# Loading the first two x tiles as two short-row loads instead of one long-row load, with one dummy product fewer and w2 in one load

## The chip, the cores and the metric

The kernel runs on one core of one Trainium2 chip. The metric is the device time of one execution in microseconds (us). Times are medians of several executions; beside them stand profiles of single executions, whose span runs from the first to the last instruction and is about 1.8 us shorter than the device time. The kernel before took 179.77 us (median of 3, 179.62 to 179.87).

## The reference, cut to what matters

For 2048 tokens of width 512 the output is `g * a + (1 - g) * b`. Here `g` is a sigmoid gate, `a` is linear attention over 32 heads, and `b` is a gated feed-forward block. The change touches only the start of the attention branch.

```python
x = A_x                                      # 1 x 2048 x 512, bf16
qkv = x @ wqkv                               # q, k, v
pq, pk = phi(q), phi(k)                      # phi(t) = where(t > 0, t + 1, exp(t)) + 1e-6
kv = einsum("bhsd,bhse->bhde", pk, v)        # sum over ALL tokens
z  = einsum("bhsd->bhd", pk)
# ... a = (pq @ kv) / (pq . z) @ wo ;  b = (silu(x @ w1) * (x @ w3)) @ w2
```

The sum over all tokens comes first: nothing of the output can be finished before k of every token has been computed and accumulated. So the kernel begins with x, its transpose xT, and the key weights wk.

## The kernel before

The kernel cuts the tokens into 16 tiles of 128. For tiles 0 and 1, TensorE transposes x through PSUM, and VectorE and ScalarE copy the result into xT. All other tiles get xT from transposing loads. While the first loads are under way, TensorE runs dummy products.

```python
    TF = 2
    x_first = x2d[0 : TF * P, :].rearrange("(p j) d -> p j d", j=TF)    # 2 KB rows: tokens 2p, 2p+1
    out_first = out2d[0 : TF * P, :].rearrange("(p j) d -> j p d", j=TF)
    dq.dma_start(out=x_sb[:, 0:TF, :], in_=x_first)                     # dq is the SP queue
    nc.scalar.dma_start(out=wk_sb[:, 0:2, :], in_=wqkv_r[:, 0:2, D : 2 * D])
    dq.dma_start(out=wk_sb[:, 2:4, :], in_=wqkv_r[:, 2:4, D : 2 * D])
    ...
    dq.dma_start(out=xT[:, :, TF * P : TB], in_=x2d[TF * P : TB, :], transpose=True)   # tiles 2, 3
    for tb in range(1, NTB):
        dq.dma_start(out=xT[:, :, tb * TB : (tb + 1) * TB], in_=..., transpose=True)
        x_ts = slice(TF if tb == 1 else tb * TPB, (tb + 1) * TPB)
        dq.dma_start(out=x_sb[:, x_ts, :], in_=x_r[:, x_ts, :])
    # ... then wq, the small weights, wv, w1, w3, wo
    for fcs in (slice(0, FC // 2), slice(FC // 2, FC)):
        dq.dma_start(out=w2_sb[:, fcs, :], in_=w2_r[:, fcs, :])
    ...
    emit_warm(TB, TB, TB, TB, TB, TB, P, P, P)      # dummies: six 512 wide, three 128 wide
    ...
    emit_xT(0)                                      # four transposes and two copies per tile
    emit_xT(1)
    for kc, t in ((0, 0), (1, 0), (0, 1), (1, 1), (2, 0), (3, 0)):
        emit_k_mm(k0[t], t, kc)                     # kc 0, 1: first half of wk; 2, 3: second half
    # ... rest of k of tiles 1 to 3 (16 products in all), then XP products and k of tiles 4 to 15 in turn
```

An "XP product" is the first use of k: it accumulates x against phi(k). From the first XP product on, TensorE has work all the time (in the profile it is busy for all of 9 to 173 us).

## Time and profile before

| What | Before | Where it is read |
|---|---|---|
| time | 179.77 us | executions |
| TensorE (PE) busy | 174.3 of 177.9 us | the page, part 1 |
| x landed, wk's first and second half landed | 3.62, 4.29, 5.29 us | single records of the trace: last semaphore update of each load |
| first k product, first XP product | 4.53, 8.94 us | the timeline |
| pitch of the 512-wide products, start to start | 0.427 us, from 6.46 us on 0.216 us | single records; the trace's clock record begins at 6.455 us |

These are lines of the page: span, busy time of each engine, the granted clock in 40 slices, and the engines' shares of the chain of waits that ended last.

```profile
span 177.9 us, 2476 instructions
...
PE 174.3 (98%) x883; PEld 84.2 (47%) x883; DVE 118.7 (67%) x204; ACT 65.5 (37%) x123; POOL 63.7 (36%) x80
...
PEclk9999999999999999999999999999999999999999
...
PE 98%; DVE 0%; issue 0%; DVEq 0%
...
```

TensorE bounds the kernel: it is 98% of the chain. The clock row says 9 in every slice, although the trace's own clock record begins only at 6.455 us. What precedes the first record is drawn as full speed (the first slice, up to 4.4 us, says 9 while the pitch there is 0.427 us), so the early state of the clock has to be read from the pitch of the products.

The next lines are the timeline of the first 10 us. Columns are start, duration (with merged neighbours), engine, line, operation, operands and count. "ACTq" and "SPq" are the instants at which a load is issued.

```profile
...
0.80 0.47 ACTq L83 DMA_DIRECT2D wk_sb<-in_A_wqkv_dram  x1
...
0.81 0.40 SPq L82 DMA_DIRECT2D x_sb<-in_A_x_dram  x1
...
0.84 3.04 PE L162 MATMUL warm<-const-bfloat16-1.0 128*128 128x512 bf16 x9 [0.84 <-PEq L495]
...
1.26 0.42 SPq L84 DMA_DIRECT2D wk_sb<-in_A_wqkv_dram  x1
...
1.73 1.31 SPq L87 DMA_TRANSPOSE xT<-in_A_x_dram  x1
...
3.67 1.06 PE L175 MATMUL xTp<-ident,x_sb 128*128 128x128 bf16 x8
...
4.53 4.58 PE L185 MATMUL k<-wk_sb,xT 128*128 128x512 bf16 x16
...
6.36 0.58 SPq L96 DMA_DIRECT2D x_sb<-in_A_x_dram  x1
...
8.94 1.03 PE L205 MATMUL XP<-pk_sb,x_sb 128*128 128x512 bf16 x4
...
```

The dummies hand over to the transposes at 3.67, just after x landed, and the transposes to the k products at 4.53. The table of waits of TensorE and the busy time of the stretch from 4 to 6 us follow.

```profile
...
PE warm L162 <- PEq L495: 0.8, 1, 0.8
```

### The profile page before, as it was taken

To read this page: it belongs to the slowest core of one execution; us is meant where nothing else is said; L and a number is where in the kernel's file an instruction comes from. 1 tells how busy PE (TensorE), PEld (TensorE's weight loads), DVE (VectorE), ACT (ScalarE), POOL (GpSimd) and SP (SyncE) were. 2 spreads that over 40 slices of the span, in tenths; PEclk is the share of its full clock that TensorE was granted. 3 is DMA by queue.
4 is the path that set the end of the run, shared out by engine and by line. 5 is a ranking of instruction groups with operands and counts; after the bars stand their busy time and mean duration, and the time that the engine had idled before them with its cause. 6 is when DMAs were issued, how large, how long until landed. Compare 5 with 4: busy or idle time off the path is not lost.

```text
span 177.9 us, 2476 instructions
## 1 busy us (share of the span) xinstructions
PE 174.3 (98%) x883; PEld 84.2 (47%) x883; DVE 118.7 (67%) x204; ACT 65.5 (37%) x123; POOL 63.7 (36%) x80
## 2 busy tenths in 40 slices
PE   8999999999999999999999999999999999999993
PEld 4444444474444545444454544444545444444463
DVE  0397667899999837498786375978754669776000
ACT  3542323476532333343333333242433323341222
POOL 6087765689154323262003232720032328000000
PEclk9999999999999999999999999999999999999999
DMA  5999999901005011123000111240001022200001
GB/s 169 205 306 284 291 332 371 335 18 29 10 1 116 0 44 33 44 59 88 0 0 11 37 37 37 60 90 6 0 7 63 10 66 63 59 0 0 29 34 58
DMA packets 30252, 15.14 MB, mean 85 GB/s; under 512 B 20672, under 2 KB 30112, under 8 KB 30240
## 3 DMA queue, kind: packets, MB, share of 16 engines
q1 hardware_dynamic: 29968, 14.72, 30.2%
q10 hardware_dynamic: 272, 0.26, 0.4%
q8 instruction: 7, 0.11, 0.3%
q14 instruction: 5, 0.04, 0.1%
HBM read 8.42 MB, written 2.10 MB: 59 GB/s over the span
## 4 chain that ended last, share of the span: by engine, by line
PE 98%; DVE 0%; issue 0%; DVEq 0%
PE o_ps L360 19%; PE up_ps L321 19%; PE gate_ps L313 19%; PE o_ps L351 8%; PE q_ps L218 8%; PE XP L205 8%; PE k_ps L185 6%; PE r_ps L242 3%; PE k L185 2%; PE o_ps L355 2%; PE warm L162 2%; PE kvT_ps L437 1%; PE W_ps L455 0%; PE xTp L175 0%; DVE o_out L369 0%
## 5 line engine op out<-in xcount | busy, mean ns | idle before, releaser
L321 PE MATMUL up_ps<-xT,w_sb 128*128 128x512 bf16 x160 | 41.1, 379 | 0.0
L313 PE MATMUL gate_ps<-xT,w_sb 128*128 128x512 bf16 x160 | 41.1, 379 | 0.0
L226 POOL TENSOR_TENSOR qz<-pq,z_sb 128x512 f32<-128x512 bf16 x16 | 18.5, 1164 | 58.1 <-DVE pq L146 58.0
L326 ACT ACTIVATE th<-gate_ps 128x512 bf16<-128x512 f32 x40 | 23.9, 597 | 39.0 <-PE gate_ps L313 37.5
L360 PE MATMUL o_ps<-w_sb,hT 128*128 128x512 bf16 (+3 forms) x180 | 37.5, 355 | 0.0
L328 DVE SCALAR_TENSOR_TENSOR gs<-th,gate_ps 128x512 bf16<-128x512 bf16 x40 | 27.2, 681 | 5.4 <-ACT th L326 5.1
L333 DVE TENSOR_TENSOR hT<-up_ps,gs 128x512 bf16<-128x512 f32 x40 | 27.6, 691 | 3.8
L143 DVE TENSOR_SCALAR phi_m<-phi_e 128x512 bf16<-128x512 bf16 x32 | 13.6, 425 | 21.8 <-ACT phi_e L141 21.6
L360 PEld LDWEIGHTS <-hT 128*128 128x128 bf16 x180 | 16.9, 98 | 17.8
L321 PEld LDWEIGHTS <-w_sb 128*128 128x128 bf16 x160 | 15.7, 98 | 18.9
L313 PEld LDWEIGHTS <-w_sb 128*128 128x128 bf16 x160 | 15.6, 98 | 18.6
L365 ACT ACTIVATE o_out<-o_ps,omg 128x512 bf16<-128x512 f32 (+2 forms) x17 | 11.2, 659 | 30.6 <-PE o_ps L360 30.6
L293 POOL TENSOR_TENSOR pqn<-pq,rden 128x512 bf16<-128x512 bf16 x16 | 16.6, 1056 | 15.0 <-DVE rden L286 13.1
L195 POOL TENSOR_TENSOR pks<-pks,pk_sb 128x512 f32<-128x512 f32 x15 | 17.4, 1161 | 7.4 <-DVE pk_sb L146 6.7
L351 PE MATMUL o_ps<-W_sb,pqT 128*128 128x512 bf16 (+3 forms) x72 | 16.8, 355 | 0.0
L218 PE MATMUL q_ps<-wq_sb,xT 128*128 128x512 bf16 x64 | 16.4, 379 | 0.0
L205 PE MATMUL XP<-pk_sb,x_sb 128*128 128x512 bf16 x64 | 16.3, 379 | 0.0
L229 DVE TENSOR_REDUCE den<-qz 128x32 f32<-128x512 f32 x16 | 10.9, 684 | 7.9 <-POOL qz L226 7.8
L141 ACT ACTIVATE phi_e<-k_ps 128x512 bf16<-128x512 f32 x12 | 7.2, 597 | 14.4 <-PE k_ps L185 14.4
L141 ACT ACTIVATE phi_e<-q_ps 128x512 bf16<-128x512 f32 x16 | 9.6, 597 | 7.8 <-PE q_ps L218 7.8
L185 PE MATMUL k_ps<-wk_sb,xT 128*128 128x512 bf16 x48 | 12.3, 379 | 0.0
L146 DVE SCALAR_TENSOR_TENSOR pq<-q_ps,phi_m 128x512 bf16<-128x512 f32 x16 | 11.1, 691 | 0.5
(59 smaller groups left out, 119.8 us busy)
## 6 DMA issues: line engine op xcount, KB each, us to landing
w_sb<-in_B_w_dram SPq DMA_DIRECT2D x6, 640.0 KB, 8.5
out_dram<-o_out SPq DMA_DIRECT2D x15, 128.0 KB, 1.7
x_sb<-in_A_x_dram SPq DMA_DIRECT2D x2, 512.0 KB, 3.9
x_sb<-in_A_x_dram SPq DMA_DIRECT2D x1, 768.0 KB, 5.1
wq_sb<-in_A_wqkv_dram SPq DMA_DIRECT2D x1, 512.0 KB, 5.1
wv_sb<-in_A_wqkv_dram SPq DMA_DIRECT2D x1, 512.0 KB, 6.3
wo_sb<-in_A_wo_dram SPq DMA_DIRECT2D x1, 512.0 KB, 9.6
wk_sb<-in_A_wqkv_dram ACTq DMA_DIRECT2D x1, 256.0 KB, 3.5
```

Source lines behind the costliest of these rows:

```text
L185: nc.tensor.matmul(k_ps[:], lhsT=xT[:, kc, t * P : (t + 1) * P], rhs=wk_sb[:, kc, :], start=(kc == 0), stop=(kc == KC - 1),)
L195: nc.gpsimd.tensor_add(pks[:], pks[:], pk_sb[:, t, :])
L205: nc.tensor.matmul(XP_ps[dc][:], lhsT=x_sb[:, t, dc * P : (dc + 1) * P], rhs=pk_sb[:, t, :], start=(t == 0), stop=(t == NT - 1),)
L218: nc.tensor.matmul(q_ps[:], lhsT=xT[:, kc, ts_tok], rhs=wq_sb[:, kc, :], start=(kc == 0), stop=(kc == KC - 1),)
L226: nc.gpsimd.tensor_tensor(out=qz[:], in0=st[tb, "pq"][:, tt, :], in1=z_sb[:], op=ALU.mult)
L313: nc.tensor.matmul(gate_ps[:], lhsT=w1_sb[:, kc, fsl], rhs=xT[:, kc, tok_sl], start=(kc == 0), stop=(kc == KC - 1),)
L321: nc.tensor.matmul(up_ps[:], lhsT=w3_sb[:, kc, fsl], rhs=xT[:, kc, tok_sl], start=(kc == 0), stop=(kc == KC - 1),)
L326: nc.scalar.activation(out=th[:], in_=gate_ps[:], func=ACT.Tanh, scale=0.5)
L328: nc.vector.scalar_tensor_tensor(out=gs[:], in0=th[:], scalar=1.0, in1=gate_ps[:], op0=ALU.add, op1=ALU.mult)
L333: nc.vector.tensor_tensor(out=st[tb, "hT"][:, fc, :], in0=up_ps[:], in1=gs[:], op=ALU.mult)
L351: nc.tensor.matmul(o_ps[:], lhsT=st[tb, "pqT"][:, c, tsl], rhs=W_sb[:, c, a:b], start=(c == 0), stop=False,)
L360: nc.tensor.matmul(o_ps[:], lhsT=st[tb, "hT"][:, fc, tsl], rhs=w2_sb[:, fc, a:b], start=False, stop=(fc == FC - 1),)
```

## The change

The intent is to let TensorE start on tile 0 while tile 1 is still in flight, in natural token order, so that the output needs no special row order. One dummy is dropped because work comes sooner, and w2 becomes one load. The diff, cut to its core:

```diff
-    dq.dma_start(out=x_sb[:, 0:TF, :], in_=x_first)
+    for t in range(TF):
+        dq.dma_start(out=x_sb[:, t, :], in_=x_r[:, t, :])
...
-    for fcs in (slice(0, FC // 2), slice(FC // 2, FC)):
-        dq.dma_start(out=w2_sb[:, fcs, :], in_=w2_r[:, fcs, :])
+    dq.dma_start(out=w2_sb[:], in_=w2_r)
...
-    emit_warm(TB, TB, TB, TB, TB, TB, P, P, P)
+    emit_warm(TB, TB, TB, TB, TB, P, P, P)
...
-                rows = out_first[t] if t < TF else out2d[t * P : (t + 1) * P, :]
+                rows = out2d[t * P : (t + 1) * P, :]
```

More of the change, by code (lines that the diff above doesn't have):

```diff
@@ L79 @@
     TF = 2
-    x_first = x2d[0 : TF * P, :].rearrange("(p j) d -> p j d", j=TF)
-    out_first = out2d[0 : TF * P, :].rearrange("(p j) d -> j p d", j=TF)
-    dq.dma_start(out=x_sb[:, 0:TF, :], in_=x_first)
+    for t in range(TF):
+        dq.dma_start(out=x_sb[:, t, :], in_=x_r[:, t, :])
     nc.scalar.dma_start(out=wk_sb[:, 0:2, :], in_=wqkv_r[:, 0:2, D : 2 * D])
```

## The prediction

> **What bounds the kernel.** TensorE. The page has PE busy 174.3 of 177.9 us (98%), and the chain that ended last is 98% PE. No wait of a matrix product is listed except the 0.8 us before the first dummy. From about 9 us on, products follow each other every 0.216 us (the chain: four in 0.86 us). So only the head, before that stream, can move the time. The stores of tiles 0 and 1 and the w2 loads are off the chain: w2 is issued at 24.4 us, lands some 8.5 us later and is first used near 58 us.
>
> **The head before** (single records of the trace). Dummies run from 0.84 us, 0.427 us apart; the last narrow one starts at 3.57. The x load is issued at 0.81 and its last semaphore update lands at 3.62; the first transpose's weight load starts at 3.66, so nothing is idle. Eight transposes take 0.107 each; the first k product starts at 4.53. Its wk half landed at 4.29; the other half lands at 5.29 and is used at 6.24. Pitch is 0.427 us until about 6.45 us and 0.216 us after: the clock was released there, although the page's clock row shows 9 in every slice. [...] So k products started earlier than 6.45 us run at half speed: moving the head by d moves the end by d/2.
>
> **What changes.** One wide dummy fewer: -0.427 us, so the dummies end near 3.25 instead of 3.68. Tile 0's load is half as large. In the packets, 2 KB took 84 ns and 1 KB 46 ns, the first up to 0.6 us; the slow engines should end tile 0 near 2.72, and with 0.35 to 0.4 us from semaphore packet to landing it is there at about 3.1: in time for 3.25. Tile 1 is issued 0.45 us later, and I expect its packets after wk's first half (from the ACT queue): before, wk's second half, issued at 1.26, sent nothing until 3.71, when the ACT queue's packets ended. [...] Estimate for slow engines: 2.72 + 16x0.046 + 8x0.046 + 0.4 = 4.2 us. So PE transposes tile 0 at 3.25 to 3.68, idles about 0.55 us, transposes tile 1 at 4.25 to 4.68 and starts k at 4.68, 0.15 us later than before. Half of it counts: +0.07 us. wk's first half would land earlier (near 3.9) and help nothing; the second half and the transposing loads come about as before. w2 in one load and contiguous stores of tiles 0 and 1: 0.
>
> **Prediction.** 179.85 us, 8 in 10 within 179.6 to 180.4. Faster by over 2%: 0.005; within 2%: 0.985; slower by over 2%: 0.01.
>
> **What would show it.** Landing of x tile 0 near 3.1 and of tile 1 near 4.2, after wk's first half; a PE gap of about 0.5 us between the fourth and fifth transpose; first k product near 4.7; pitch change still at 6.4 to 6.5; from 10 us on the same stream, shifted by under 0.1 us; w2 lands long before 58 us.
>
> **What would make it wrong.** [...] (2) Tile 1's packets go before wk's: it lands near 3.6, k starts with wk at about 4.3, and the kernel is 0.1 us faster; chance 0.3. (3) A later transposing load for tiles 2 and 3 (slack about 0.35 us at 7.0 us) opens a small gap.

## More of the kernel before

Behind "4.00:6.00" and the length stand the busy times of PE, PEld, DVE, ACT and POOL, then clock, DMA share and GB/s.

```profile
...
4.00:6.00 2.00, 2.00 (x11) 1.12 (x10) 0.58 (x2) 0.77 (x2) 0.00 (x0) 1.00 1.16 250
...
```

PE waits only for its start, and the DMA queues moved 250 GB/s in that stretch.

## The result, and the profile after

The changed kernel took 179.58 us (median of 6, 179.26 to 179.97), the kernel before 179.69 us (median of 6, 179.01 to 179.89). The ratio is 1.000 with a 95% interval of 0.9978 to 1.0022: the same. A ratio here is the mean time of one kernel's fast runs over that of the other's in the same rounds, so it is not quite the ratio of the medians quoted.

The same parts of the page, after:

```profile
span 178.0 us, 2458 instructions
...
PE 173.0 (97%) x866; PEld 83.8 (47%) x882; DVE 118.7 (67%) x204; ACT 65.5 (37%) x123; POOL 63.9 (36%) x80
...
PEclk9999999999999999999999999999999999999999
...
PE 94%; DMA 3%; issue 1%; SPq 0%; DVE 0%; DVEq 0%
...
```

The chain now holds 3% of DMA: 2.5% is the load of wk's second half. (PE counts 17 products fewer, but PEld only one weight load fewer, which is the dummy: the other 16 are records missing from the trace.) The timeline of the changed kernel:

```profile
...
0.80 0.46 ACTq L82 DMA_DIRECT2D wk_sb<-in_A_wqkv_dram  x1
...
0.81 0.87 SPq L81 DMA_DIRECT2D x_sb<-in_A_x_dram  x2
...
0.84 2.61 PE L160 MATMUL warm<-const-bfloat16-1.0 128*128 128x512 bf16 x8 [0.84 <-PEq L493]
...
1.73 0.43 SPq L83 DMA_DIRECT2D wk_sb<-in_A_wqkv_dram  x1
...
2.19 1.69 SPq L86 DMA_TRANSPOSE xT<-in_A_x_dram  x1
...
3.25 0.63 PE L173 MATMUL xTp<-ident,x_sb 128*128 128x128 bf16 x4
...
4.20 0.61 PE L173 MATMUL xTp<-ident,x_sb 128*128 128x128 bf16 x4 [0.32 <-DMA x_sb<-in_A_x_dram]
...
4.60 1.50 PE L183 MATMUL k<-wk_sb,xT 128*128 128x512 bf16 x4
...
6.27 2.92 PE L183 MATMUL k<-wk_sb,xT 128*128 128x512 bf16 x12 [0.17 <-DMA wk_sb<-in_A_wqkv_dram]
...
6.99 0.58 SPq L95 DMA_DIRECT2D x_sb<-in_A_x_dram  x1
7.29 1.41 PEld L183 LDWEIGHTS <-xT 128*128 128x128 bf16 x8 [0.49 <-DMA xT<-in_A_x_dram]
...
```

The transposes fall into two groups of four (3.25 and 4.20), the k products into a group of four at 4.60 and the other twelve from 6.27, and the weight load for the ninth k product starts only at 7.29. The table of waits names three:

```profile
...
PE warm L160 <- PEq L493: 0.8, 1, 0.8
PE xTp L173 <- DMA x_sb<-in_A_x_dram: 0.3, 1, 0.3
PE k L183 <- DMA wk_sb<-in_A_wqkv_dram: 0.2, 1, 0.2
```

The same stretch from 4 to 6 us shows that the DMA queues slowed down just there, to 135 GB/s:

```profile
...
4.00:6.00 2.00, 1.80 (x8) 0.95 (x9) 0.29 (x1) 0.69 (x2) 0.00 (x0) 1.00 1.18 135
...
```

| Step (us) | Before | Predicted | After |
|---|---|---|---|
| x tile 0 landed / tile 1 landed | 3.62 together | 3.1 / 4.2 | 3.09 / 4.15 |
| wk's first half landed | 4.29 | 3.9 | 3.79 |
| first k product | 4.53 | 4.68 | 4.60 |
| wk's second half landed | 5.29 | about as before | 6.23 |
| xT of tiles 2 and 3 landed | 6.64 | about as before | 7.25 |
| pitch changes | 6.46 | 6.4 to 6.5 | 5.55 |
| first XP product | 8.94 | about 9.0 | 9.03 |
| last PE instruction minus first XP product | 165.99 | same | 165.99 |

The first XP product is where I had put it, but not by my sum: that it came out right was luck. The pitch changed 0.9 us earlier than before, a gain of about 0.45 us, and TensorE stood still for wk (0.34 us) and xT (0.16 us), a loss of about the same size. The last row says that nothing after the first XP product changed: neither w2 in one load nor the output rows cost or gave anything.

### The profile page after: what moved, and what is told of

Same layout as the page of the kernel before. It is cut to its first block, busy times and chain, and to the rows that moved or that the text cites. A ratio compares the mean times of both kernels' runs of the same rounds, so it can differ in the third digit from the quotient of the medians.

```text
span 178.0 us, 2458 instructions
## 1 busy us (share of the span) xinstructions
PE 173.0 (97%) x866; PEld 83.8 (47%) x882; DVE 118.7 (67%) x204; ACT 65.5 (37%) x123; POOL 63.9 (36%) x80
## 3 DMA queue, kind: packets, MB, share of 16 engines
HBM read 8.42 MB, written 2.10 MB: 59 GB/s over the span
## 4 chain that ended last, share of the span: by engine, by line
PE 94%; DMA 3%; issue 1%; SPq 0%; DVE 0%; DVEq 0%
PE o_ps L358 19%; PE up_ps L319 19%; PE gate_ps L311 19%; PE o_ps L349 8%; PE XP L203 8%; PE q_ps L216 8%; PE k_ps L183 6%; PE r_ps L240 3%; DMA wk_sb<-in_A_wqkv_dram 3%; PE o_ps L353 2%; PE k L183 2%; PE kvT_ps L435 1%; PE W_ps L453 0%; SPq L81 0%; DVE o_out L367 0%
```

## The experiments

Twelve runs of nine kernels were made. All gave correct results. Those of one job shared a chip and the runs of the kernel before.

### The kernel before against itself, and the changed kernel again

Theory P: the instant of the pitch change (call it R) is not the kernel's own. Rival K: it follows the kernel's work. Theory C: the DMA stall comes with the change. Rival A: it was an accident of one execution. Neither kernel was edited.

> The kernel before, unchanged, run against itself: what two sets of the same program differ by. Theory P (phase): the moment at which the pitch of the products falls from 0.427 to 0.216 us does not belong to the kernel; it was 6.455 us in the profile of before and 5.548 us in that of after, and it will be elsewhere again here, by up to a few us, while x lands at 3.6 and the first k product starts at 4.53 as before. Rival K (kernel): the moment follows the kernel's own work, and it is again 6.45 us within 0.05. Time: ratio 1.000, within 0.3%.

> The changed kernel, unchanged. In its profile the second half of wk landed at 6.23 us (5.29 before) because packets of the transposing load stood for up to 1.38 us, and PE waited 0.34 us for wk and 0.16 us for xT. Theory C: that stall comes with the change (wk third on the SP queue, the transposing load right behind it), so wk's second half lands after 6.0 us again. Rival A (accident): it lands near 5.3 us and no packet of the first transposing load takes over 0.5 us. In both: x tile 0 lands near 3.1, tile 1 near 4.15, first k product near 4.6. Time: ratio to before 1.000 within 0.3% under A; up to 0.3% slower under C when the pitch changes early.

Measured: the kernel before against itself took 179.45 us (6 runs) against 178.94 us (11 runs), ratio 1.0017 (0.9993 to 1.004). So the same program differs from itself by half a microsecond in its medians on one chip. The changed kernel took 179.63 us, ratio 1.0031 (1.0013 to 1.005). Timelines of TensorE, the kernel before first:

```profile
...
3.89 1.03 PE L175 MATMUL xTp<-ident,x_sb 128*128 128x128 bf16 x8
4.72 4.10 PE L185 MATMUL k<-wk_sb,xT 128*128 128x512 bf16 x16
8.65 1.03 PE L205 MATMUL XP<-pk_sb,x_sb 128*128 128x512 bf16 x4
...
```

```profile
...
3.25 0.63 PE L173 MATMUL xTp<-ident,x_sb 128*128 128x128 bf16 x4
4.36 0.61 PE L173 MATMUL xTp<-ident,x_sb 128*128 128x128 bf16 x4 [0.48 <-DMA x_sb<-in_A_x_dram]
4.76 3.80 PE L183 MATMUL k<-wk_sb,xT 128*128 128x512 bf16 x16
8.40 1.03 PE L203 MATMUL XP<-pk_sb,x_sb 128*128 128x512 bf16 x4
...
```

R lay at 5.68 us in the first and 5.13 us in the second. It had been 6.46 in the first profile of before, and it came earlier although the kernel's own work came later (x landed at 3.84 instead of the expected 3.6, k at 4.72 instead of 4.53): P stands and K falls. The clock records also show a grid. The time from the release of the clock (granted share 1.0 from 6.455 us in before) to the fall at the end (share 0.5 from 177.122 us) is 170.666 us in before, and 174.079 us in after and in both kernels here; these differ by 3.413 us and are 50 and 51 times 3.4133 us. So in these four profiles both changes of the clock lie on one grid of 3.4133 us, and as the same program met it at different instants (R at 6.46 and 5.68 us), the kernel does not set it. One step of this grid, 3.413 us, is called a window below.

With R known, the head can be summed. A k product started before R takes 0.427 us, one after R 0.216 us, and there are 16. So the first XP product starts at `R + 3.453 - 0.506 * (R - k)`, where k is the first k product, if PE waits for nothing in between (if R comes before k, at `k + 3.453`):

| Profile | k | R | sum | measured | PE waits |
|---|---|---|---|---|---|
| before | 4.53 | 6.46 | 8.93 | 8.94 | none |
| before, second | 4.72 | 5.68 | 8.65 | 8.65 | none |
| after | 4.60 | 5.55 | 8.52 | 9.03 | 0.34 for wk, 0.16 for xT |
| after, second | 4.76 | 5.13 | 8.40 | 8.40 | none |

The waits of "after" here are gaps between product starts in single records: the fifth started at 6.27 instead of 5.94, the ninth at 7.29 instead of 7.13. The sum holds to 0.01 us, and what it lacks is exactly the waits. The second profile of the changed kernel shows no stall. Its wk landed at 5.29, its xT at 6.43, and the stretch from 4 to 6 us moved 265 GB/s:

```profile
...
4.00:6.00 2.00, 1.64 (x9) 0.95 (x10) 0.29 (x1) 0.69 (x2) 0.00 (x0) 1.00 1.20 265
...
```

So the stall is not in every execution, as rival A said; whether the change makes it more frequent was still open.

### The split alone, and the dummy alone

```diff
 # the split alone: the kernel before with
-    dq.dma_start(out=x_sb[:, 0:TF, :], in_=x_first)
+    for t in range(TF):
+        dq.dma_start(out=x_sb[:, t, :], in_=x_r[:, t, :])
 # (and the output rows of tiles 0 and 1 in natural order)
 # the dummy alone: the kernel before with
-    emit_warm(TB, TB, TB, TB, TB, TB, P, P, P)
+    emit_warm(TB, TB, TB, TB, TB, P, P, P)
```

> The kernel before with the x load split alone: six wide dummies and two w2 loads stay. The dummies end near 3.68, so tile 0 is transposed at 3.68 to 4.1 although it landed near 3.1; tile 1 lands near 4.15 and is transposed at once; first k product near 4.6, as in the changed kernel. So if tile 1's landing is the bound, keeping the dummy costs nothing: same time as the changed kernel (within 0.1 us at the same moment of the pitch change). If the dummies were the bound instead, k would start near 5.0.

> The kernel before with one wide dummy fewer alone. x lands at 3.62 as before, so PE stands idle from about 3.25 to 3.66 and the first k product starts at 4.53 as before: the dummy was filler, 0.00 us. If idleness counted against the clock, the pitch change would come at least a window of about 3.4 us later than in a run of before with the same phase (k products still 0.427 us apart at 8 us).

The dummy alone: 179.19 us, ratio 1.0012 (0.9993 to 1.0032). Its TensorE timeline:

```profile
...
0.84 2.61 PE L162 MATMUL warm<-const-bfloat16-1.0 128*128 128x512 bf16 x8 [0.84 <-PEq L495]
3.85 1.04 PE L175 MATMUL xTp<-ident,x_sb 128*128 128x128 bf16 x8 [0.40 <-DMA x_sb<-in_A_x_dram]
4.68 4.36 PE L185 MATMUL k<-wk_sb,xT 128*128 128x512 bf16 x16
...
```

From the end of the dummies (3.25, by the starts of the products) to the first transpose (3.85) PE idled 0.60 us: 0.43 for the missing dummy, the rest because x landed only at 3.81 in this execution (3.62 was expected). The transposes began at once, and the k products followed them without a pause. The second profile of the kernel before, where x landed at 3.84, has its first k product at 4.72, so the missing dummy cost nothing: it was filler. By the starts of the products the pitch changed at about 6.2 us, so 0.60 us of idleness did not hold the clock back here.

The split alone: 180.10 us, ratio 1.0064 (1.0043 to 1.0084), the slowest of the four and not as expected. Its timeline has three stalls and a fourth at 12.7 us:

```profile
...
3.68 0.48 PE L174 MATMUL xTp<-ident,x_sb 128*128 128x128 bf16 x4
4.31 0.40 PE L174 MATMUL xTp<-ident,x_sb 128*128 128x128 bf16 x4 [0.15 <-DMA x_sb<-in_A_x_dram]
4.54 1.04 PE L184 MATMUL k<-wk_sb,xT 128*128 128x512 bf16 x4
5.79 1.02 PE L184 MATMUL k<-wk_sb,xT 128*128 128x512 bf16 x4 [0.20 <-DMA wk_sb<-in_A_wqkv_dram]
7.03 1.90 PE L184 MATMUL k<-wk_sb,xT 128*128 128x512 bf16 x8 [0.22 <-DMA xT<-in_A_x_dram]
8.77 1.03 PE L204 MATMUL XP<-pk_sb,x_sb 128*128 128x512 bf16 x4
...
```

```profile
...
12.72 1.04 PE L204 MATMUL XP<-pk_sb,x_sb 128*128 128x512 bf16 x3 [0.34 <-DMA x_sb<-in_A_x_dram]
```

The first k product started at 4.54, as expected, and R was 3.86, very early. The sum would put the first XP product at 8.00; it started at 8.77. The fourth stall, for x of tiles 2 to 7, cost another 0.5 us: from the first XP product to the last PE instruction it took 166.50 us instead of 165.99. All four are late loads.

Single DMA records show what they have in common. A 256-byte packet of a transposing load takes 0.018 us (the median over the first 9 us in before and in after). In the two profiles with the stall so far, and in a third one below, many packets of the first transposing load took over 0.5 us, and they ended together, about 0.2 us after the last packet of wk's second half (in after they took 0.59 to 1.38 us):

| Profile | packets over 0.5 us | the longest | all ended between | wk's last packet ended |
|---|---|---|---|---|
| after | 19 | 1.38 us | 5.97 and 6.01 us | 5.80 us |
| after, third | 22 | 1.01 us | 5.78 and 5.83 us | 5.60 us |
| the split alone | 14 | 0.90 us | 5.52 and 5.56 us | 5.36 us |

In after, 13 of 16 semaphore packets of wk's second half had gone out by 4.44 us, but all but one of their updates arrived only from 6.04 us on. Their load was late too (xT of tiles 2 and 3 landed at 7.25 us in after, at 6.64 in before). Why these packets took so long was not shown. In the first profile of before the updates of wk's second half also came bunched, from 5.05 us on, 0.2 us after its last packet (4.83 us). So what differs in the stalled profiles is how late the last packets of wk's second half are: in after, its last three semaphore packets went out at 4.88, 5.62 and 5.80 us. In the other profiles of this job, and in the first one of before, no such packet took longer than 0.35 us.

### Which part makes the split slow: dummy or w2

```diff
 # the changed kernel with
-    emit_warm(TB, TB, TB, TB, TB, P, P, P)
+    emit_warm(TB, TB, TB, TB, TB, TB, P, P, P)
 # w2 alone: the kernel before with
-    for fcs in (slice(0, FC // 2), slice(FC // 2, FC)):
-        dq.dma_start(out=w2_sb[:, fcs, :], in_=w2_r[:, fcs, :])
+    dq.dma_start(out=w2_sb[:], in_=w2_r)
```

> The changed kernel with the sixth wide dummy put back (so: split x loads and one w2 load). On the last chip the split alone (six dummies, two w2 loads) took 180.1 us against 179.6 of the changed kernel and 178.9 of before. Theory D: the dummy makes the difference between those two, so this one takes as long as the split alone, 0.6% over before. Rival W: the single w2 load makes it, so this one is as fast as the changed kernel, 0.3% over before. Rival L (lag): neither does; what costs is one engine that starts the second half of wk late, behind which all packets of the first transposing load stand. Then the profile shows, when slow, packets of that load above 0.5 us, xT of tiles 2 and 3 after 6.9 us and a PE wait for it, and when fast, none.

> The kernel before with w2 in one load alone. w2 is issued after 24 us, lands in the thirties and is first used near 58 us, so 0.00 us: ratio 1.000 within 0.2%, and PE without a gap from 12 to 58 us. Theory W of the run above would need this to be faster by 0.2 to 0.3%.

The changed kernel with six dummies took 179.39 us against 179.64, ratio 1.0001 (0.9973 to 1.003). w2 alone took 179.39 us, ratio 0.9999 (0.9973 to 1.0026). Neither profile has a stall (wk landed at 5.13 and 5.34), and both have 165.99 us behind the first XP product. Theory D (the dummy) falls. Theory W (w2) would have needed w2 alone to be faster; it was not. Theory L, a lag in some executions, is what is left, by elimination and not by a test: the split alone was 0.6% over before in both its sets, this kernel, which differs from it in the w2 load only, in its one set was not, and a joint effect of the split and the two w2 loads was not ruled out (w2 is issued at 24 us, long after the head).

### The order of the first loads

```diff
 # tile 1 on the ACT queue: the changed kernel with
-    for t in range(TF):
-        dq.dma_start(out=x_sb[:, t, :], in_=x_r[:, t, :])
+    dq.dma_start(out=x_sb[:, 0, :], in_=x_r[:, 0, :])
+    nc.scalar.dma_start(out=x_sb[:, 1, :], in_=x_r[:, 1, :])
 # one load of short rows: the kernel before with
-    dq.dma_start(out=x_sb[:, 0:TF, :], in_=x_first)
+    dq.dma_start(out=x_sb[:, 0:TF, :], in_=x_r[:, 0:TF, :])
 # (and the output rows of tiles 0 and 1 in natural order)
```

> The changed kernel with tile 1 issued from the ACT queue, before wk's first half; on the SP queue wk's second half and the transposing loads come one issue (0.46 us) sooner. Theory O (order): tile 1 lands near 3.5 instead of 4.15 to 4.3, because nothing stands before it; wk's first half lands near 4.2 and now bounds, first k product near 4.3 (4.6 to 4.76 in the changed kernel); SP issues as in before. Rival: the ACT queue's packets come as late as they did for wk, after those of x tile 0 and wk's second half, and tile 1 lands after 4 us again. Time: as before or up to 0.15 us less at the same moment of the pitch change; against the changed kernel 0.2 to 0.5 us less if its cost was the SP queue's order.

> The kernel before with one x load in natural token order: 256 rows of 1 KB instead of 128 of 2 KB, one issue. Tells the size of the rows from the number of loads. By the packet times (46 ns for 1 KB, 84 for 2 KB) the load takes 16 x 46 instead of 8 x 84 ns per engine, 0.06 us more: lands near 3.7, first k product at 4.6, time +0.03 us, within 0.1% of before. If short rows are what makes an engine lag, packets of the first transposing load stand for over 0.5 us here too and the time is 0.3 to 0.6% over before, as with the split.

Tile 1 on the ACT queue took 181.80 us, ratio 1.0115 (1.0077 to 1.0153), so the expectation of a faster kernel was a miss. Its tile 1 landed at 3.79 and tile 0 at 3.61, together nearly as late as the one long-row load. wk's first half, now second on the ACT queue, landed last of all, at 5.63, after the second half at 5.44, and the first k product started at 5.67. TensorE stood idle for 1.3 us. Five of its six executions took 181.5 to 182.0 us; the profiled one took 179.8, with R at 4.22 (three packets of its first transposing load took 0.51 to 0.56 us).

One load of short rows took 180.05 us, ratio 1.0026 (1.0001 to 1.0052). It landed at 4.27 instead of the expected 3.7; wk's packets on the ACT queue went out among its own from 2.3 us on. It had no lag (no packet of the first transposing load above 0.42 us). Its sum, with k at 5.15 and R at 6.31, gives 9.18, and 9.18 was measured. So short rows cost 0.6 us here where the packet times said 0.06; that the other queue's load took its share in between is the likely reason, and was not tested apart.

### All of the head on one queue, and repeats

```diff
 # the changed kernel with
-    nc.scalar.dma_start(out=wk_sb[:, 0:2, :], in_=wqkv_r[:, 0:2, D : 2 * D])
+    dq.dma_start(out=wk_sb[:, 0:2, :], in_=wqkv_r[:, 0:2, D : 2 * D])
```

> The changed kernel with wk's first half on the SP queue too, so that nothing competes: x tile 0, x tile 1, wk first half, wk second half. Theory Q: tile 1 was late because the ACT queue's wk packets went between the two tiles. Then tile 1 lands near 3.5, wk's halves near 4.2 and 5.2, first k product near 4.3, and no engine starts late (no packet of the first transposing load over 0.5 us). Everything behind on the SP queue is issued one more issue (0.46 us) later, so xT of tiles 2 and 3 may land near 6.8 and be waited for when the pitch changes early. Time: within 0.15% of before; if the 0.46 us per issue is what costs, 0.1 to 0.3% slower than before.

> Tile 1 on the ACT queue once more, one look. Five of its six executions took 181.5 to 182.0 us, the profiled one 179.8 with the pitch change at 4.22 us and a PE gap of 1.1 us before the first k product. Theory G (gap): in the slow ones the gap kept the clock from being released, and the pitch changes one window later. If this execution is slow (over 181), its k and first XP products stand 0.427 us apart until after 7 us. Rival: it is slow by a DMA that lands 2 us late, with the pitch change before 6.5 us as elsewhere.

With all four loads on the SP queue, tile 0 landed at 2.93 and tile 1 at 3.40: theory Q about their order is right. All eight transposes ran at once. But wk's first half landed at 5.24 instead of 4.2: twelve of its 16 semaphore updates had arrived by 4.48, the last four came from 4.87 on. Two packets of the first transposing load took 0.56 us, where none over 0.5 was expected. So late parts of a load occur here too, with no other queue in between, and why stays open. The time was 181.41 us, ratio 1.0104 (1.0067 to 1.014), with executions in two groups: 179.8 and 180.0, and four at 181.4 to 182.0. The profiled execution was one of the slow group (181.52). TensorE's timeline:

```profile
...
3.25 1.06 PE L173 MATMUL xTp<-ident,x_sb 128*128 128x128 bf16 x8
5.28 5.72 PE L183 MATMUL k<-wk_sb,xT 128*128 128x512 bf16 x16 [0.97 <-DMA wk_sb<-in_A_wqkv_dram]
10.84 1.03 PE L203 MATMUL XP<-pk_sb,x_sb 128*128 128x512 bf16 x4
...
```

TensorE idled from 4.10 to 5.28, and its 16 k products then took 5.72 us against 4.58 before: R was 9.58. On the grid, the clock could have been released one window earlier, at 6.17, but the 3.413 us up to there held the gap of 1.18 us. By the sum, R at 6.17 gives a first XP product at 9.17; it started at 10.84, so 1.7 us later. The repeated look at tile 1 on the ACT queue, meant to catch a slow execution of that kernel, caught a fast one (179.56 us, R at 3.94), so for that kernel the cause of the slow group is likely the same but was not recorded.

From the profiles one can read how busy TensorE was in the window that ended at R and in the one before it (share of 3.413 us between product starts, idle gaps taken out):

| Profile | R | last window | window before it |
|---|---|---|---|
| before | 6.46 | 1.00 | 0.64 |
| after | 5.55 | 0.85 | 0.38 |
| after, second | 5.13 | 0.80 | 0.25 |
| after, third | 3.65 | 0.81 | 0.00 |
| all on SP | 9.58 | 1.00 | 0.66 |

In these profiles a window with 0.80 sufficed and one with 0.66 did not. The shares count the transposes: the 0.80 of "after, second" would be 0.56 without them, and it released the clock, while the 0.64 of before, dummies alone, did not. Transposes started 0.107 us apart before R (before) and about 0.06 us after it (the split alone, 4.31 to 4.49 us). The gap between the two tiles was 0.52 us in the first profile of the changed kernel and 0.69 us in the second, where it leaves 0.80: enough, but not by much.

> The split alone once more (six dummies, two w2 loads): 0.64% over before on one chip, while the same with w2 in one load showed 0.0% on another. Theory L (an engine that lags in some executions, or on some chips): the ratio is anywhere from 1.000 to 1.006, and goes with the profile: packets of the first transposing load over 0.5 us when slow, none when fast. Rival D/W (program): 0.6% over before again.

> The changed kernel a third time, beside the split alone on the same chip: theory L says that the two differ by no more than the lag does, so within 0.3% of each other if neither or both lag. First XP product, by the sum found so far (moment of the pitch change + 3.453 - 0.506 x (that moment - first k product)) within 0.02 us unless PE waits for wk or xT.

In the last job, the split alone took 180.01 us, ratio 1.0055 (1.0033 to 1.0077), and the changed kernel 179.85 us, ratio 1.0045 (1.0021 to 1.0069), the kernel before 179.04 us. The two are within 0.3% of each other, as theory L says. The profiles differ. The split alone had no packet above 0.46 us, but tile 1 landed at 4.57 and k started at 5.02; sum 8.81, measured 8.82. The changed kernel lagged again: packets of up to 1.01 us, wk's second half at 6.06, xT at 7.06; with R at 3.65 the sum without waits is 8.05, measured 8.84. The expectation for the split alone, that its ratio goes with the lag, holds only in part: this profile was slow without one, by a late tile 1.

### What ten profiles say together

One can take the landing times of each profile, replay the 16 k products with them (0.427 us before R, 0.216 after, the fifth waiting for wk, the ninth for xT), and average over R from 3.2 to 6.65 us. That range is an estimate: it is where a window first is at least 0.7 busy if PE starts at 0.84 (0.7 lies between the 0.66 that did not release the clock and the 0.80 that did). The replay gives the measured first XP product within 0.02 us in the profiles with a recorded R. Averaged, it is 8.52, 8.44, 8.46 and 8.39 us for the four profiles with one long-row load (before twice, dummy alone, w2 alone; mean 8.45), and 9.02, 8.47, 8.84, 8.40, 8.77 and 8.67 us for the six with the split (mean 8.70). So the split costs about 0.25 us as an estimate free of R, with the stall in three of six profiles against none of four. Replayed without the waits for wk and xT, the two means are 8.36 and 8.42: about 0.05 us of the cost is the later start of k, close to the 0.07 predicted, and the rest is the waits. (The fourth stall of the split alone, 0.5 us at 12.7 us, is not in these numbers.) The timed ratios of the changed kernel in its three sets were 1.000, 1.003 and 1.0045; the means differ by 0.01, 0.57 and 0.71 us.

No experiment points to a version that beats the kernel before.

## Why the prediction was right or wrong

- **The verdict was right.** No difference beyond 2%, and the time 0.27 us from the figure given. It lies 0.02 us below the low end of the range as written; the two later sets of the same kernel (179.63 and 179.85 us) lie inside it. Since the kernel before differs from itself by half a microsecond, this says little about the steps, and a hit here is in part luck: in the profile, R 0.9 us earlier gained 0.45 us and the waits for wk and xT cost 0.5. So the steps have to be judged singly.
- **Landings and first k product: right.** Tile 0 at 3.09 (predicted 3.1), tile 1 at 4.15 (4.2), after wk's first half at 3.79 (3.9), a PE gap of 0.52 us (0.5), first k product at 4.60 (4.68). That the ACT queue's load goes between the two tiles was confirmed by taking it away: tile 1 then landed at 3.40.
- **"Moving the head by d moves the end by d/2": right while R is later than the k products.** The sum shows a factor of 0.506 to 0.01 us in the executions without waits. It is 1, not 1/2, when R comes before the first k product: in both profiles of tile 1 on the ACT queue (k at 5.67 and 5.40, R at 4.22 and 3.94) the first XP product came 3.45 us after k.
- **"Pitch change still at 6.4 to 6.5": wrong.** I took R of one profile for a property of the kernel. It lay anywhere from 3.65 to 6.46 us in all profiles but one (9.58), on a grid of 3.413 us that the kernel does not set. Each microsecond of R is worth 0.49 us, which is several times the 0.07 us that I predicted, so profile against profile could not be compared without correcting for it.
- **"The second half and the transposing loads come about as before": wrong.** In three of six profiles with the split, wk's second half landed 0.5 to 0.9 us late and PE waited for wk and xT, in sum 0.5 to 0.8 us. I had named a late transposing load as risk (3), as a small gap. This is the term that was mis-sized: +0.07 us in my sum, about +0.25 us over the profiles.
- **The PE gap: it did not delay the clock in the profiles of the changed kernel.** The first two, with gaps of 0.52 and 0.69 us, had windows 0.85 and 0.80 busy at R. Where the gap was 1.18 us (all on SP, that window 0.66 busy), R came at 9.58 instead of 6.17 and it cost 1.7 us.
- **w2, the dummy and the output rows at zero: right.** w2 alone and the dummy alone stand at 0.9999 and 1.0012, and behind the first XP product every profile but the first of the split alone has 165.99 us.

Open: what makes one or two of the 16 semaphore packets of wk's second half so late when the lag occurs ("one engine" is a reading: the DMA records carry no engine number), and whether the split causes it or only meets it more often. Three of six against none of four is suggestive and not proof.

## What to carry to other kernels

Before comparing two profiles of a head that runs before the clock is released, read from the pitch (0.427 against 0.216 us here) where it was released in each, and correct for it; the instant was not the kernel's (6.46 and 5.68 us in two profiles of one program). An extra load at the front of a queue is not only its own bytes: what another queue slipped in between decided here when it landed (tile 1 at 4.15 us with wk's first half in between, at 3.40 without), and the loads behind it came late in three of six profiles with the split (wk's second half at 6.23 us in after, 5.29 in before). Idle time in the head did not delay the release where the window stayed 0.80 busy, and went with a release one window of 3.413 us later where it was 0.66 busy.
